# Sigmoid attention and a SiLU feed-forward: a scores-first option for visits, new orders for the opening, for FF1's products and for the places of visits

## The chip, the cores and the metric

The kernel runs on one core of a Trainium2 chip. What counts is the device time of one execution in microseconds, as the median of several runs. The core has five engines with an instruction stream each: PE (matmuls; PEld are its weight loads), DVE (vector), ACT (activations), POOL and SP (both issue DMAs here; POOL also computes). They run beside each other and wait for one another through semaphores only.

## The reference

```python
# q, k, v: (8 batches, 12 heads, 448 positions, 64)
scores = scale * np.matmul(q, k.transpose(0, 1, 3, 2)) - np.log(S)
attn = 1.0 / (1.0 + np.exp(-scores))
x = np.matmul(attn, v)            # then to (3584 tokens, 768)
h = x @ w_in                      # (768, 2048)
g = h * (1.0 / (1.0 + np.exp(-h)))
out = g @ w_out                   # (2048, 768)
```

The sigmoid takes the place of a softmax, so no row sums are needed. The kernel holds its operands in float16 and accumulates in float32.

## The kernel before

Attention is cut into 24 groups `i` of four heads, three for each batch (`i = 3*batch + n`). Each group has seven score steps `r` of 64 keys. A score step (`score_step`, L172) is four 64x64 matmuls of 448 columns that fill the four quadrants of PE, and gives one PSUM pair of banks; `sigmoid` (L178, ACT) brings it to SBUF as float16. The values of a group (`value_steps`, L188) are 7 x 4 such matmuls and read all seven sigmoids; `to_x` (L206 on DVE; L203 and L204 on DVE and ACT for the last group of batch 1) moves the result into x. In the code a unit `("s", i, r)` is a score step with its sigmoid, and `("a", i)` is a group's values with the move. The three PSUM pairs are `att0`, `att1`, `att2`; two single banks `ffp0` and `ffp1` form "pair 3".

A *visit* is a short run of such units put into the stream of feed-forward matmuls. `visit` takes the pairs that have been unused for longest, first does the "a" units, and then the "s" units; it also fires the loads and transpositions of groups to come. A score step needs its pair to have been emptied by the sigmoid, or by the move, that used it last.

The program runs in this order.

1. *Opening* (the list `INIT`). Loads, transpositions of q and k on PE (`T`, L148, copied out by DVE at L158), the scores of batch 0 and the first of batch 1, the values of batch 0 in pieces (`V`, one piece for each step), the moves to x (`X`), and the first FF1 matmuls (`F n`: n of them). `("s",)` is the next score step; these alternate between `att0` and `att1`. `("L", kind, i)` is a load by POOL's queue (kind 0 q, 1 k, 2 v; two DMAs each), `("W", s)` a quarter of w_in by the same queue. POOL has at most eight loads open at a time: each issue waits for the landing of the one eight before it. The quarters are called W0 to W3 below; FF1 needs W0 from step 0, W1 from step 24, W2 from step 48, W3 from step 72.
2. *FF1 of batch 0* (`ff1_first`, L282): 96 matmuls in eight blocks of 12, alternately in pair 3 and `att2`; after each block ACT's sigmoid (L295, L299) and a DVE multiply (L297, L300) make the gate. The list `PROGRAM` gives the steps (0 to 96) at which visits ("v") of two units stand, and where DVE forms the sums of w_in ("w", L317 to L319; "l", L323) and of x ("x" and "y", L218) that a Strassen-like scheme needs.
3. *Phases 1 to 7*. Phase `b` first does `ff1` of batch b (L350): 14 products of 12 matmuls, seven for each half `s` of the columns. `ORD[b-1]` says in which order the two halves take turns. Within a half the products alternate between two pairs X and Z; a product can start when the one before in its pair has been copied out (ACT, L381), added up (DVE, L385) or gated. Then comes the second matrix product, `ff2` (L473): 88 to 144 matmuls, through `ffp0` and `ffp1`. `PHASES[b-1]` lists the step among them at which each visit of batch b+1 stands, and how many units it has (2 or 3 near the end, 1 for the last group's values). The last visit brings the x that the next phase's FF1 begins with.

With visits of 3, 3, 3, 3, 3, 3, 3, 2, 1 units, visits 0, 1, 2, 4 and 5 hold scores only, visits 3 and 6 hold values and scores, and the last holds values only. The order is written out by hand: every engine takes its instructions in the order in which the code emits them.

```python
pairs = [p for p in used if p < n][: len(us)]
for p in pairs:
    used.remove(p)
    used.append(p)
```

Of the kernel before, what the change touches and what calls it, by code (L numbers as in the profile page):

```python
# [16 lines left out]
def kernel(  # L17
# [149 lines left out]
    def score_step(i, r, pair):  # L167
        qT, kT = qk_of(i)
        for e, j in ((0, 0), (1, 1), (0, 1), (1, 0)):
            re = slice(e * HP, (e + 1) * HP)  # L170
            cj = slice(j * HP, (j + 1) * HP)
            nc.tensor.matmul(  # L172
                att[pair][cj, e, :S], kT[re, r, cj], qT[re, :, cj], start=True, stop=True
            )
# [54 lines left out]

    used = [0, 1, 2]  # L230

    def visit(us, n=3, hold=False):

        if not hold:
            flush()
        pairs = [p for p in used if p < n][: len(us)]
        for p in pairs:
            used.remove(p)
            used.append(p)
        for u in us:  # L240
            if u[0] == "a":
                pr = pairs.pop(0)
                value_steps(u[1], pr, range(R))
                to_x(u[1], pr, hold)
                if u[1] >= 2 * NQ:
                    x_sums(slice(u[1] % NQ, u[1] % NQ + 1))
        for u in us:
            if u[0] == "s":
                pr = pairs.pop(0)
                score_step(u[1], u[2], pr)  # L250
                sigmoid(u[1], u[2], pr)
        for u in us:
            for f in events.pop(u, ()):
                f()
# [357 lines left out]
    def T(kind, i, pair):  # L612
# [3 lines left out]
            t_copy(kind, i, pair, half, dve)  # L616

    PROGRAM = (
# [6 lines left out]
    )  # L625

    INIT = (
# [13 lines left out]
    )  # L641

    us = units_of(1)
    scores = [("s", i, r) for i in range(NQ) for r in range(R)] + us
    ns = 0
    for what, *a in INIT:
        if what == "s":
            u = scores[ns]
# [17 lines left out]
    us = us[ns - NQ * R :]  # L666
# [25 lines left out]
    for n, kind, c in PROGRAM:  # L692
        ff0_steps(n - done)
        done = n
        if kind == "v":
            visit(vs[vn], 2, vn == len(vs) - 1)
            vn += 1
        else:
            acts[kind, c]()
# [1 line left out]


    PHASES = (
# [6 lines left out]
        (),  # L710
    )

# [3 lines left out]
    )  # L716

    ORD = (
# [7 lines left out]
    )  # L726

    FF2 = (
# [5 lines left out]
    for b in range(1, B):  # L734
# [15 lines left out]
        it = run()  # L750
        done = 0
        nu = 0
        for target, m in PHASES[b - 1]:
            while done < target:
                next(it)
                done += 1
            visit(us[nu : nu + m])
            nu += m
        for _ in it:
            pass  # L760
# [30 lines left out]
```

## Time and profile before

| | us |
|---|---|
| median of 4 runs | 371.49 (371.34 to 371.89) |
| the profiled execution's own time | 371.58 |
| its span from first to last instruction | 369.8 |
| opening, up to the first FF1 matmul | 0 to 30.1 |
| FF1 of batch 0 and its visits | 30.1 to 60.0 |
| phase 1 | 60.0 to 106.2 |
| phases 2, 3, 4 | 44.3 each, to 239.2 |
| phase 5 | 42.3, to 281.6 |
| phase 6 | 44.5, to 326.0 |
| phase 7 and the end | 43.8, to 369.8 |

The boundaries are the starts of each stage's first matmul in PE's timeline. Busy times come from the profiled execution, which is one run; so estimates are made against its own 371.58 us. In a timeline, the first column is the start in us, the second how long the merged run of instructions lasts, x4 how many they are, and the brackets how long the engine had been idle and what released it. The ends of matmuls are modelled and overlap the next ones, so the time that a matmul takes is read from the start of the next one.

### The profile page before, as it was taken

The page shows a single profiled execution, that of the slowest core. Times are in us where ns is not written, and L with a number is a line of the kernel's source. Part 1 is how long each engine was busy: PE and PEld are TensorE (multiplying, and loading weights), DVE is VectorE, ACT ScalarE, POOL GpSimd, SP SyncE. Part 2 cuts the span into 40 slices and gives each one's busy share as a digit, 9 for nine tenths or more (in the row PEclk, how much of TensorE's full clock was granted, in tenths as well). Part 3 has the DMA queues.
Part 4 walks back from the last instruction along what each step waited for, and adds up shares of the span by engine and source line. Part 5 has one row for each costly group of instructions (what it writes and reads, how often), then busy time and mean ns, then how long its engine had stood idle before and what let it go on. Part 6 is the DMA issues. An engine that isn't in the chain of part 4 may idle for free.

```text
span 369.8 us, 8711 instructions
## 1 busy us (share of the span) xinstructions
PE 357.2 (97%) x3594; PEld 238.9 (65%) x3594; DVE 223.1 (60%) x399; ACT 256.2 (69%) x291; POOL 159.6 (43%) x162
## 2 busy tenths in 40 slices
PE   7779999999999999999999999999999999999995
PEld 3444446965579655895549955598547965489663
DVE  2673688958765574665655755627366557436762
ACT  3989897778846797577875778467994779746100
POOL 8871430295305923169121872029631590006500
PEclk9999999999999999999999999999999999999999
DMA  8999999859897099662997449891799715130133
GB/s 145 169 178 205 228 226 188 149 124 129 143 267 158 6 171 211 162 151 38 205 183 172 101 56 203 203 209 28 102 177 225 152 17 118 29 87 2 43 87 85
DMA packets 64839, 51.13 MB, mean 138 GB/s; under 512 B 36896, under 2 KB 61728, under 8 KB 64800
## 3 DMA queue, kind: packets, MB, share of 16 engines
q1 hardware_dynamic: 48544, 35.24, 44.3%
q0 software_dynamic: 15328, 14.32, 26.6%
q10 hardware_dynamic: 928, 1.02, 0.9%
q8 instruction: 28, 0.46, 0.6%
q14 instruction: 11, 0.09, 0.1%
HBM read 45.61 MB, written 11.01 MB: 153 GB/s over the span
## 4 chain that ended last, share of the span: by engine, by line
PE 88%; ACT 5%; DVE 3%; issue 1%; DMA 1%; POOL 0%; ACTq 0%; DVEq 0%; POOLq 0%
PE ffp L473 35%; PE att L350 24%; PE att L172 9%; PE att L188 9%; PE ffp L350 6%; ACT attnT L178 5%; PE att L282 2%; PE ffp L282 2%; DMA st<-in_q_dram 1%; DVE wt L158 1%; DVE qkT L158 1%; PE att L148 0%; PE ffp L148 0%; DVE gT L300 0%; DVE gT L373 0%
## 5 line engine op out<-in xcount | busy, mean ns | idle before, releaser
L178 ACT ACTIVATE attnT<-att,bias_s 128x896 f16<-128x896 f32 x168 | 157.4, 1008 | 28.1 <-PE att L172 27.5
L371 POOL TENSOR_TENSOR gT<-attnT,gT 128x896 f16<-128x896 f32 x42 | 77.9, 1885 | 54.3 <-ACT gT L369 54.3
L126 POOL CAST st<-st 128x896 f16<-128x896 f32 x36 | 33.6, 952 | 120.2 <-DMA st<-in_k_dram 53.9
L350 PEld LDWEIGHTS <-w_in_sb 128*128 128x128 f16 x672 | 64.4, 98 | 1.6 <-issue 0.8
L350 PE MATMUL att<-xT,w_in_sb 128*128 128x224 f16 x588 | 61.2, 259 | 0.3 <-DVE gT L300 0.3
L473 PEld LDWEIGHTS <-gT 128*128 128x128 f16 x416 | 39.1, 98 | 28.7 <-issue 5.3
L381 ACT COPY attnT<-att 128x896 f32<-128x896 f32 x35 | 31.7, 906 | 37.4 <-PE att L350 37.1
L473 PEld LDWEIGHTS <-gs 128*128 128x128 f16 x384 | 34.8, 98 | 32.0 <-issue 11.5
L473 PE MATMUL ffp<-w_out_sb,gT 128*128 128x384 f16 x288 | 51.5, 326 | 0.0
L369 ACT ACTIVATE gT<-attnT 128x896 f16<-128x896 f32 x42 | 39.9, 951 | 16.2 <-DVE attnT L385 14.9
L350 PEld LDWEIGHTS <-sw 128*128 128x128 f16 x504 | 48.3, 98 | 0.1
L172 PE MATMUL att<-qkT,qkT 64*64 64x448 f16 x588 | 41.9, 358 | 4.3 <-ACT attnT L178 3.2
L385 DVE TENSOR_TENSOR attnT<-att,attnT 128x896 f32<-128x896 f32 x28 | 30.5, 1092 | 17.1 <-PE att L350 16.1
L206 DVE TENSOR_SCALAR xT<-att 128x896 f16<-128x896 f32 x21 | 22.9, 1091 | 26.5 <-PE att L188 26.5
L473 PE MATMUL ffp<-w_out_sb,gs 128*128 128x384 f16 x192 | 36.3, 327 | 0.0
L473 PE MATMUL ffp<-wt,gs 128*128 128x384 f16 x192 | 35.8, 327 | 0.0
L484 DVE TENSOR_SCALAR snap<-ffp 128x384 f32<-128x384 f32 x40 | 22.2, 555 | 21.3 <-PE ffp L473 21.3
L350 PE MATMUL att<-xT,sw 128*128 128x224 f16 x336 | 35.0, 259 | 0.0
L188 PE MATMUL att<-attnT,v 64*64 64x448 f16 x588 | 32.7, 352 | 1.3 <-DVE wt L158 0.9
L172 PEld LDWEIGHTS <-qkT 64*64 64x64 f16 x588 | 16.9, 105 | 24.4 <-issue 18.3
L487 DVE SCALAR_TENSOR_TENSOR osb<-ffp,snap 128x384 f32<-128x384 f32 x40 | 22.2, 554 | 17.2 <-PE ffp L473 17.0
L385 DVE TENSOR_TENSOR attnT<-ffp,attnT 128x448 f32<-128x448 f32 x28 | 16.1, 617 | 25.7 <-PE ffp L350 14.4
(72 smaller groups left out, 339.0 us busy)
## 6 DMA issues: line engine op xcount, KB each, us to landing
out_dram<-osb SPq DMA_DIRECT2D x48, 192.0 KB, 3.8
st<-in_k_dram SPq DMA_DIRECT2D x36, 224.0 KB, 5.0
st<-in_q_dram SPq DMA_DIRECT2D x36, 224.0 KB, 5.2
v<-in_v_dram POOLq DMA_DIRECT2D x44, 112.0 KB, 4.3
w_in_sb<-in_moe_w_in_dram POOLq DMA_DIRECT2D x4, 768.0 KB, 12.5
w_out_sb<-in_moe_w_out_dram POOLq DMA_DIRECT2D x4, 768.0 KB, 18.6
sw<-in_k_dram POOLq DMA_DIRECT2D x8, 112.0 KB, 4.3
sw<-in_q_dram POOLq DMA_DIRECT2D x8, 112.0 KB, 4.3
```

The lines of the kernel that those rows point to most:

```text
L126: nc.gpsimd.tensor_copy(st16[kind].rearrange("p r e d -> p e r d"), st32[kind].rearrange("p e (r d) -> p e r d", r=R),)
L172: nc.tensor.matmul(att[pair][cj, e, :S], kT[re, r, cj], qT[re, :, cj], start=True, stop=True)
L178: nc.scalar.activation(attnT[:, s0 : s0 + 2, :], att[pair][:, :, :S], AF.Sigmoid, bias=bias_s, scale=QKSCALE)
L188: nc.tensor.matmul(bank(pair, j)[e * HP : (e + 1) * HP, :S], vt[rj, e, r, :], attnT[rj, s0 + e, :], start=(r == 0), stop=(r == R - 1),)
L206: nc.vector.tensor_scalar_mul(x, att[pair][:, :, :S], SX)
L350: nc.tensor.matmul(o, a[:, c, (4 * s + f) * P : (4 * s + f + 1) * P], xb[:, c], start=first and c == 0 and f % 2 == 0, stop=c == KC - 1, s ...
L369: nc.scalar.activation(oo, ap, AF.Sigmoid, bias=0.0, scale=ISX)
L371: nc.gpsimd.tensor_mul(oo, ap, oo)
L381: nc.scalar.copy(as2(h[:, i, c], ap), ap)
L385: nc.vector.tensor_add(as2(h[:, i, c], ap), ap, as2(h[:, i, c], ap))
L473: nc.tensor.matmul(bank, a[:, fc], w[:, fc], start=first and fc == 0, stop=fc == KH - 1, skip_group_check=True,)
L484: nc.vector.tensor_scalar_mul(snap[i], bank, ISX)
```

## The change

`visit` gets an argument `scores_first`; with it the "s" units of a visit are emitted before its "a" units, and take the pairs in that order. A new table `SF` lists the visits that are to have it: `SF[0]` for the visits of `PROGRAM`, `SF[b]` for those of phase b. `INIT`, `PROGRAM`, `PHASES` and `ORD` get new entries; the instructions are the same in kind and number. In the opening the loads are in a different order as well (q of unit 4 ahead of its k, q of unit 5 ahead of a v load, the v load of unit 3 ahead of W1). The order of SP's queue is the same.

```diff
-    def visit(us, n=3, hold=False):
+    def visit(us, n=3, hold=False, scores_first=False):
...
-        for u in us:
-            if u[0] == "a":
+        for what in ("s", "a") if scores_first else ("a", "s"):
+            for u in us:
+                if u[0] != what:
+                    continue
                 pr = pairs.pop(0)
+                if what == "s":
+                    score_step(u[1], u[2], pr)
+                    sigmoid(u[1], u[2], pr)
+                    continue
...
     PROGRAM = (
-        (8, "v", 0), (16, "v", 0), (32, "v", 0), (38, "v", 0), (43, "w", 1),
-        (43, "v", 0), (51, "v", 0), (53, "w", 0), (58, "v", 0), (69, "v", 0),
-        (71, "w", 3), (74, "v", 0), (86, "w", 2), (89, "v", 0), (94, "v", 0),
-        (96, "l", 1), (96, "x", 0), (96, "v", 0), (96, "x", 1), (96, "x", 2),
-        (96, "f", 0), (96, "l", 0), (96, "y", 2), (96, "y", 1), (96, "y", 0),
+        (14, "v", 0), (20, "v", 0), (28, "v", 0), (36, "w", 1), (37, "v", 0),
+        (43, "v", 0), (52, "v", 0), (58, "w", 0), (59, "v", 0), (64, "v", 0),
+        (67, "w", 3), (72, "v", 0), (86, "v", 0), (93, "v", 0), (93, "w", 2),
+        (96, "x", 0), (96, "l", 1), (96, "v", 0), (96, "x", 1), (96, "x", 2),
+        (96, "y", 0), (96, "y", 2), (96, "f", 0), (96, "y", 1), (96, "l", 0),
         (96, "1", 0), (96, "2", 0),
     )
+    SF = (
+        (0, 1, 2, 3, 6, 7, 9, 10, 11), (2, 5, 7, 10), (0, 1, 2, 5), (0, 1, 2, 7, 10),
+        (1, 2, 5, 7), (4, 5, 7, 8, 9), (1, 2), (),
+    )
     INIT = (
-        ("L", 1, 3), ("s",), ("s",), ("T", 1, 1, 2), ("s",), ("s",), ("s",),
-        ("T", 0, 1, 3), ("L", 0, 3), ("L", 1, 4), ("s",), ("T", 1, 2, 2), ("s",),
-        ("L", 0, 4), ("s",), ("T", 0, 2, 3), ("s",), ("L", 2, 1), ("L", 1, 5),
-        ("T", 1, 3, 2), ("s",), ("V", 0, 2, 0), ("V", 0, 2, 1), ("s",), ("L", 2, 2),
-        ("V", 0, 2, 2), ("L", 0, 5), ("W", 0), ("W", 1), ("V", 0, 2, 3), ("V", 0, 2, 4),
-        ("T", 0, 3, 3), ("V", 0, 2, 5), ("s",), ("V", 0, 2, 6), ("X", 0, 2),
-        ("T", 1, 4, 3), ("s",), ("s",), ("W", 2), ("T", 0, 4, 2), ("s",), ("L", 2, 5),
-        ("V", 1, 3, 0), ("V", 1, 3, 1), ("L", 2, 4), ("L", 2, 3), ("s",), ("s",),
-        ("W", 3), ("T", 1, 5, 2), ("s",), ("V", 1, 3, 2), ("T", 0, 5, 2),
-        ("V", 1, 3, 3), ("s",), ("V", 1, 3, 4), ("V", 1, 3, 5), ("s",), ("s",),
-        ("V", 2, 2, 0), ("V", 2, 2, 1), ("V", 2, 2, 2), ("V", 2, 2, 3), ("V", 1, 3, 6),
-        ("s",), ("V", 2, 2, 4), ("V", 2, 2, 5), ("V", 2, 2, 6), ("s",), ("X", 1, 3),
-        ("F", 4), ("X", 2, 2, True), ("F", 4),
+        ("s",), ("s",), ("s",), ("T", 1, 1, 2), ("L", 1, 3), ("s",), ("L", 0, 3),
+        ("T", 0, 1, 3), ("s",), ("s",), ("T", 1, 2, 2), ("s",), ("s",), ("L", 0, 4),
+        ("T", 0, 2, 3), ("L", 1, 4), ("s",), ("L", 2, 1), ("T", 1, 3, 2),
+        ("T", 0, 3, 3), ("s",), ("L", 1, 5), ("V", 0, 2, 0), ("L", 0, 5), ("s",),
+        ("V", 0, 2, 1), ("L", 2, 2), ("V", 0, 2, 2), ("V", 0, 2, 3), ("W", 0),
+        ("L", 2, 3), ("V", 0, 2, 4), ("V", 0, 2, 5), ("V", 0, 2, 6), ("W", 1), ("W", 2),
+        ("s",), ("s",), ("X", 0, 2), ("s",), ("T", 1, 4, 3), ("T", 0, 4, 2), ("s",),
+        ("L", 2, 5), ("V", 1, 3, 0), ("V", 1, 3, 1), ("W", 3), ("s",), ("V", 1, 3, 2),
+        ("T", 1, 5, 2), ("s",), ("s",), ("T", 0, 5, 2), ("V", 1, 3, 3), ("s",),
+        ("V", 1, 3, 4), ("s",), ("V", 1, 3, 5), ("V", 2, 2, 0), ("V", 2, 2, 1), ("s",),
+        ("L", 2, 4), ("V", 2, 2, 2), ("V", 1, 3, 6), ("V", 2, 2, 3), ("V", 2, 2, 4),
+        ("s",), ("V", 2, 2, 5), ("s",), ("V", 2, 2, 6), ("X", 1, 3), ("F", 4), ("F", 4),
+        ("X", 2, 2, True),
     )
...
-            visit(vs[vn], 2, vn == len(vs) - 1)
+            visit(vs[vn], 2, vn == len(vs) - 1, vn in SF[0])
...
     PHASES = (
-        ((19, 3), (33, 3), (46, 3), (58, 3), (67, 3), (82, 3), (90, 3), (97, 2), (107, 1)),
-        ((19, 3), (33, 3), (47, 3), (53, 3), (62, 3), (77, 3), (89, 2), (95, 3), (107, 1)),
+        ((19, 3), (33, 3), (47, 3), (55, 3), (67, 3), (82, 3), (89, 3), (100, 2), (106, 1)),
+        ((19, 3), (33, 3), (47, 3), (53, 3), (63, 3), (78, 3), (85, 2), (93, 3), (108, 1)),
         ((19, 3), (33, 3), (48, 3), (54, 3), (63, 3), (77, 3), (85, 3), (91, 2), (98, 1)),
-        ((17, 3), (32, 3), (46, 3), (53, 3), (62, 3), (76, 3), (83, 3), (92, 2), (97, 1)),
-        ((14, 3), (23, 3), (37, 3), (40, 3), (47, 3), (58, 3), (63, 2), (67, 3), (75, 1)),
-        ((19, 3), (32, 3), (44, 3), (50, 3), (59, 3), (75, 3), (83, 3), (91, 2), (99, 1)),
+        ((18, 3), (32, 3), (47, 3), (54, 3), (63, 3), (77, 3), (84, 3), (92, 2), (99, 1)),
+        ((18, 3), (31, 3), (43, 3), (46, 3), (53, 3), (64, 3), (68, 2), (73, 3), (81, 1)),
+        ((18, 3), (32, 3), (45, 3), (51, 3), (60, 3), (74, 3), (85, 3), (92, 2), (99, 1)),
         (),
     )
     ORD = (
-        (0, 0, 1, 0, 1, 1, 0, 0, 1, 0, 1, 0, 1, 1),
-        (0, 0, 1, 1, 0, 0, 1, 0, 0, 1, 1, 0, 1, 1),
-        (0, 1, 0, 0, 1, 1, 0, 0, 1, 1, 0, 0, 1, 1),
-        (0, 0, 1, 0, 0, 1, 1, 0, 1, 1, 0, 0, 1, 1),
-        (0, 0, 1, 1, 0, 1, 0, 0, 1, 0, 1, 0, 1, 1),
-        (0, 0, 1, 1, 0, 1, 0, 1, 0, 0, 1, 0, 1, 1),
-        (0, 0, 1, 1, 0, 0, 1, 0, 1, 0, 1, 0, 1, 1),
+        (0, 0, 0, 1, 1, 1, 0, 0, 1, 1, 0, 0, 1, 1),
+        (0, 0, 1, 1, 0, 1, 0, 0, 0, 1, 1, 0, 1, 1),
+        (0, 1, 0, 0, 1, 0, 1, 1, 0, 1, 0, 0, 1, 1),
+        (0, 0, 1, 0, 0, 1, 1, 0, 1, 0, 1, 0, 1, 1),
+        (0, 0, 1, 1, 0, 1, 0, 1, 0, 1, 0, 0, 1, 1),
+        (0, 1, 0, 0, 1, 0, 1, 1, 0, 1, 0, 0, 1, 1),
+        (0, 0, 1, 0, 1, 0, 0, 1, 0, 1, 1, 0, 1, 1),
     )
...
-            visit(us[nu : nu + m])
+            visit(us[nu : nu + m], scores_first=nv in SF[b])
```

The step at which a visit stands counts FF1 matmuls in `PROGRAM` and FF2 matmuls in `PHASES`.

More of the change, by code (lines that the diff above doesn't have):

```diff
@@ L246, in visit @@
                     x_sums(slice(u[1] % NQ, u[1] % NQ + 1))
[L247 to L251, printed above, removed]
         for u in us:
@@ L752 @@
         nu = 0
-        for target, m in PHASES[b - 1]:
+        for nv, (target, m) in enumerate(PHASES[b - 1]):
             while done < target:
```

## The prediction

> **What bounds the kernel now.** I read the page's busy row first, then the windows of the stretches between the stages, then PE's and ACT's timelines in the stretches where PE is not full.
>
> ```profile
> PE 357.2 (97%) x3594; PEld 238.9 (65%) x3594; DVE 223.1 (60%) x399; ACT 256.2 (69%) x291; POOL 159.6 (43%) x162
> ```
>
> PE is busy nearly throughout, but a busy PE is not PE at its peak, so stages are compared:
>
> ```profile
> 7.90:30.10 22.20, 17.36 (x317) 10.18 (x317) 13.40 (x24) 19.98 (x22) 16.36 (x28) 1.00 1.18 176
> 30.10:60.00 29.90, 29.14 (x260) 12.87 (x256) 19.56 (x32) 26.27 (x34) 8.83 (x12) 1.00 1.19 218
> 194.90:239.20 44.30, 44.30 (x450) 30.66 (x448) 27.01 (x50) 32.25 (x36) 20.11 (x18) 1.00 0.74 148
> 239.20:281.60 42.40, 41.70 (x427) 28.95 (x425) 21.91 (x41) 32.23 (x36) 20.13 (x18) 1.00 0.72 138
> ```
>
> Columns after the length: busy PE, PEld, DVE, ACT, POOL. Phase 4 (third line) is pure PE. Phases 2, 3 and 4 last 44.3 us each and hold the same matmuls: nothing is to be gained there, only lost. The opening (first line) is ACT's: 20.0 of 22.2 us. Phase 5 has the same 21 sigmoids on ACT but 24 FF2 matmuls fewer (88 for 112), so its PE waits. Where:
>
> ```profile
> 257.69 0.57 PE L172 MATMUL att<-qkT,qkT 64*64 64x448 f16 x8
> 258.43 0.38 PE L172 MATMUL att<-qkT,qkT 64*64 64x448 f16 x4 [0.17 <-DVE gT L373]
> ...
> 260.32 0.57 PE L172 MATMUL att<-qkT,qkT 64*64 64x448 f16 x8
> 261.05 0.38 PE L172 MATMUL att<-qkT,qkT 64*64 64x448 f16 x4 [0.16 <-ACT attnT L178]
> ```
>
> A score step of four quadrant matmuls takes 0.19-0.21 us start to start (258.43 would have been 258.10). The gaps in brackets look small because matmul ends are modelled; by starts the two stalls cost 0.34 and 0.33 us.
>
> ACT in the opening, and POOL's loads behind it:
>
> ```profile
> 17.69 1.01 ACT L178 ACTIVATE attnT<-att,bias_s 128x896 f16<-128x896 f32 x1 [0.31 <-PE att L172]
> 19.28 1.01 ACT L178 ACTIVATE attnT<-att,bias_s 128x896 f16<-128x896 f32 x1 [0.58 <-PE att L172]
> 20.53 5.50 ACT L178 ACTIVATE attnT<-att,bias_s 128x896 f16<-128x896 f32 x6 [0.25 <-PE att L172]
> 26.73 4.60 ACT L178 ACTIVATE attnT<-att,bias_s 128x896 f16<-128x896 f32 x5 [0.70 <-PE att L172]
> ```
> ```profile
> 19.72 2.52 POOL L554 DMA_DIRECT2D w_in_sb<-in_moe_w_in_dram  x3
> ...
> 29.91 0.60 POOL L119 DMA_DIRECT2D v<-in_v_dram  x1 [4.69 <-DMA w_in_sb<-in_moe_w_in_dram]
> 33.70 0.84 POOL L554 DMA_DIRECT2D w_in_sb<-in_moe_w_in_dram  x1 [3.20 <-DMA w_in_sb<-in_moe_w_in_dram]
> ```
>
> Back to back, sigmoids start 0.89 us apart (5.50 for six, each 1.0 long). ACT idles four times waiting for a score that PE issued late. The POOL waits date the landings of w_in's pieces: W0 29.6, W1 33.4, so 3.8 us apiece. PE's first FF1 matmul stands at 30.09, only 0.5 us after W0.
>
> **What the skill says.** "TensorE: Matmul & The Clock Gate", section "Architectural detail: the array is 16× 32×32, not 1× 128×128": PE pulls only weight loads ahead, ACT and DVE are strict FIFO; so an instruction that waits holds all behind it. The trace agrees: the waits of L172 stop the FF2 stream. "DMA: Bandwidth & Descriptors", section "Anatomy of one DMA — SWDGE (gpsimd) path", prices a transfer at 2.0 us plus bytes/436 GB/s. A w_in piece is 128x6x512 floats, 1.57 MB: 3.6 us of movement; the trace shows 3.8 between landings.
>
> **The change, part by part.**
>
> *Scores ahead of values: nothing.* The option re-orders only a visit that holds both kinds. In the batch-0 program those are visits 4 and 8; the list has 0-3, 6, 7, 9-11. In phases 1 to 6 they are visits 3 and 6; the lists (2,5,7,10), (0,1,2,5), (0,1,2,7,10), (1,2,5,7), (4,5,7,8,9), (1,2) never name them. Not one instruction moves by it.
>
> *Opening (the list INIT).* I place each score by the rules above: its bank is free 0.05 us after the sigmoid before last; its own sigmoid starts 0.43 us after it (17.26 to 17.69) or when ACT is free; a transposition pair takes 0.58 us on PE, its two copies 1.16 us on DVE. Up to s1.1 ACT runs full in both. Now both transpositions of unit 3 stand ahead of s1.2, and q's half landed only at 16.06, so s1.2 goes from 15.63 to 16.65 and its sigmoid from 16.31 to 17.07 (a new gap of 0.76). But the value steps and transpositions that delayed s1.4 by 0.58 and s2.4 by 0.70 no longer do: s1.3 17.96, s1.4 18.88, s1.5 19.77, s1.6 20.66, s2.0 21.80, s2.1 22.83, s2.2 24.06, s2.4 25.87, s3.1 29.43 instead of 30.32. ACT gains 0.9 us; PE reaches FF1 at 29.2. W0 has the same eight loads ahead of it, so it lands at about 29.6: FF1 starts at 29.65 instead of 30.09. Gain 0.44, the rest hidden by W0.
>
> *FF1 of batch 0 (the list PROGRAM).* 96 matmuls at 0.187 us; a visit of two scores costs 0.50, with values 1.9, plus 0.1 on re-entry. The first visit is now at step 14, past the first gate, so ACT does the gate first and is no further ahead at the next scores (s3.4 34.6 for 34.9). Stalls for a bank: before 0.52 (39.35 to 40.06), 0.5 (41.83), 0.27 (47.02), 0.2 (57.98); now by the same rules 0.43 (s3.5), 0.2 (a3), 0.29 (s5.0), 0.32 (s5.2). Summing from 29.65 I get steps 24, 43, 72, 96 at 35.9, 40.7, 50.5, 57.7 and the last value's end at 59.2 instead of 60.0: gain 0.85 in all with the 0.44. One more v load (0.57 us each half) goes ahead of W1, so it lands at 34.6-35.0, needed at 35.9. The DVE sums at step 36 need W2 (W1 and 3.8 us more, 38.5-38.9) and are reached at 40.7. Step 93's sums end near 58.0, before the last value.
>
> *FF1 of phase 1 (ORD).* Before:
>
> ```profile
> 61.25 1.41 PE L350 MATMUL ffp<-xT,sw 128*128 128x224 f16 x12
> 62.93 1.31 PE L350 MATMUL att<-xT,w_in_sb 128*128 128x224 f16 x12 [0.26 <-DVE gT L300]
> ```
>
> A product takes 1.15 us, here 1.68: the third one waited for batch 0's last gate multiply on DVE. Now the third product reuses its own bank after the copy (0.26 latency + 0.91 + 0.05 against 1.15: stall 0.07) and the gate's bank comes fourth. The multiply itself is moved behind four x sums (4 x 0.19), so it ends just then (0.05); "1,1,1" costs 0.07. Gain 0.25.
>
> *ORD elsewhere.* "0,0,0" in phase 2 falls on products whose bank a DVE pair of 2 x 0.62 frees, half by half: ready at 0.86 and 1.40, needed at 1.15 and 1.73. In the other orders at least two products lie between a bank's uses, or one where the evacuation is that pair. Zero; range 0 to 0.3 lost over six phases.
>
> *PHASES.* Moves of one to three steps change nothing in phases that had no stall. In phase 5 visits go 14, 23, 37, 40 ... 75 to 18, 31, 43, 46 ... 81. The first visit comes at 255.33+18x0.163+0.09 = 258.35, so DVE's multiply (end 258.38) is done when its third score comes. 13 and 12 steps (2.1, 2.0 us) plus the visit's 0.69 then cover three sigmoids (2.68 to 2.8). By the opening's rules what is left is 0.05, 0.1, 0.15+0.28 (visit 3), 0.3 (visit 5), 0.06: 0.9 us. Before, phase 5 stood 1.9 us over the loss of phases 2 to 4 (start-to-start sum less the undisturbed spacing). Gain 1.0; range 0.5 to 1.2. What is late next is the last value: 7 FF2 matmuls (1.14 us) and two thirds of the first product (0.77) cover x's move (0.2 + 1.09 + 0.05): enough by 0.6. In phase 2 the last visit at 108 leaves 0.65+0.77 = 1.42 against 1.34: enough by 0.1. Phase 6: visit 45 for 44 saves 0.1.
>
> *Sum.* 0.85+0.25+1.0 = 2.1. The profiled execution took 371.58 us (span 369.8), the median 371.49; 2.1 off either gives 369.5 and 369.4. Less than 0.2% (0.74 us) could not be told from no change.
>
> **Rivals.** (A) The opening is held by w_in. If a w_in piece behind small loads takes what W0 took (6.4 us after the load ahead of it, not 3.8), W1 lands at 30.8+6.4 = 37.2: 1.3 late at step 24, of which later stalls give back some 0.4. For it: W0's 6.4; against it: W0 had an empty transfer ahead. Gain 1.2: 370.3. (B) Phase 5 only trades stalls: ACT has 21 x 0.89 = 18.8 us of sigmoids between 258.85 and the last value at 279, 20.1 us, so 1.3 us of slack; small gaps on ACT eat it and the last value waits for its seventh sigmoid. With 0.5 gained there, 0.3 lost in ORD, 0.4 of the opening's 0.85 and nothing in phase 1: gain 0.6, 370.9. (C) Slower: W1's issue is held by the limit of eight open loads until W0 lands (as the v load at 29.91 was), and takes W0's 9.9 us from issue: 39.8, 3.9 after step 24. It decides from a landing past 38.7 (35.9+2.1+0.74) and gives 373.3. Against it: W1 is only the third after W0, its slot's former load landed at 20.9. (D) W0 itself comes earlier, since one PE wait fewer stands ahead of it: up to 0.4 more, and fewer stalls: 368.6.
>
> **How the numbers follow.** Forecast 0.58, A 0.17, B 0.13 (0.04 of it still faster by 0.2%), C 0.06, D 0.06. Faster 0.58+0.17+0.04+0.06 = 0.85, same 0.09, slower 0.06. The range goes from D's side, 368.2, to B's, 371.1.
>
> **What would show it.** FF1's first matmul at 29.6; ACT's gaps in the opening 0.76 at 16.3 and then under 0.4; the last value of batch 0 ending near 59.2; phase 1's FF1 16.4 long instead of 16.7; phases 2 to 4 still 44.3; phase 5 41.3 for 42.3. Wrong if a stall stands at step 24, if phases 2 to 4 lengthen, or if the first two stalls of phase 5 remain.

## The result and the profile after

| | median, us | runs, lowest to highest | ratio to before (95% interval) |
|---|---|---|---|
| before | 371.75 | 59, 371.17 to 374.66 | |
| changed | 370.55 | 38, 369.36 to 372.09 | 0.9964 (0.9956 to 0.9973) |

The change takes 0.36% off by the ratio, 1.3 us (the two medians lie 1.2 apart), where 2.1 was forecast. Single executions of the changed kernel spread over 2.7 us, and its profiled one, with 371.70 us (span 369.8), is among the slowest: as a whole it is no faster than the profiled one of before (371.58). So it is read stage by stage. Windows of the changed kernel, cut at its own first matmuls of each stage; after the length come the busy times of PE, PEld, DVE, ACT and POOL, then TensorE's granted clock, the DMA share and GB/s:

```profile
7.90:30.60 22.70, 18.18 (x317) 10.88 (x318) 14.08 (x25) 20.57 (x23) 16.42 (x26) 0.92 1.11 163
30.60:60.50 29.90, 29.14 (x261) 12.73 (x257) 18.33 (x31) 26.62 (x34) 8.66 (x12) 1.00 1.19 218
60.50:107.35 46.85, 46.10 (x460) 31.35 (x457) 37.46 (x66) 32.99 (x37) 20.79 (x18) 1.00 0.86 149
195.90:240.30 44.40, 44.40 (x450) 30.74 (x449) 26.80 (x50) 32.19 (x36) 20.11 (x18) 1.00 0.75 151
240.30:281.70 41.40, 41.09 (x426) 28.96 (x424) 22.10 (x40) 32.35 (x36) 20.07 (x18) 1.00 0.69 127
```

The reader is to see four things. The opening is longer than before (22.7 for 22.2), at a clock of 0.92. FF1 of batch 0 lasts 29.9 as before. Phase 1 has grown from 46.2 to 46.85. Phase 5 is down from 42.4 to 41.4. PE's timeline of phase 5 shows that its first two stalls are gone; the lines at 259.46 and 262.37 are the first two visits, their twelve matmuls in one piece each, where both were cut by a stall in the kernel before (at 258.43 and 261.05):

```profile
257.74 1.46 PE L474 MATMUL ffp<-w_out_sb,gT 128*128 128x384 f16 x8
259.04 0.49 PE L474 MATMUL ffp<-wt,gT 128*128 128x384 f16 x2
259.46 0.76 PE L172 MATMUL att<-qkT,qkT 64*64 64x448 f16 x12
260.15 1.15 PE L474 MATMUL ffp<-wt,gT 128*128 128x384 f16 x6
...
262.37 0.82 PE L172 MATMUL att<-qkT,qkT 64*64 64x448 f16 x12
```

ACT's timeline of the opening, whose gaps before were 0.31, 0.58, 0.25 and 0.70:

```profile
8.65 2.81 ACT L178 ACTIVATE attnT<-att,bias_s 128x896 f16<-128x896 f32 x3 [0.62 <-PE att L172]
11.76 1.01 ACT L178 ACTIVATE attnT<-att,bias_s 128x896 f16<-128x896 f32 x1 [0.30 <-PE att L172]
13.16 6.63 ACT L178 ACTIVATE attnT<-att,bias_s 128x896 f16<-128x896 f32 x7 [0.39 <-PE att L172]
20.10 4.91 ACT L178 ACTIVATE attnT<-att,bias_s 128x896 f16<-128x896 f32 x5 [0.32 <-PE att L172]
25.21 6.62 ACT L178 ACTIVATE attnT<-att,bias_s 128x896 f16<-128x896 f32 x7 [0.20 <-PE att L172]
```

The late gaps have shrunk as forecast (0.32 and 0.20 are left). But there are new ones at 11.76 and 13.16, where no order was meant to cost anything, and the first sigmoid is at 8.65 (before: 8.29). In the window from 9.5 to 13.0 the granted clock was 0.51 in this execution and 1.00 in that of before. The two new gaps fall under this clock: there the fourteen matmuls of a transposition took 0.96 us (the first line, of the changed kernel), where they take 0.58 in an execution at full clock (the second line, of the run `after_t_early` below), so the scores came late.

```profile
10.23 0.96 PE L148 MATMUL att<-ident,sw 128*64 128x128 f16 x14
8.60 0.58 PE L148 MATMUL att<-ident,sw 128*64 128x128 f16 x14
```

Most of the new loss in phase 1 is one stall. PE waits at step 48 of FF2 (one matmul after the visit at 47) for DVE's copy of the product that ended at step 40. The expectations below call this place step 41.

```profile
86.19 0.76 PE L172 MATMUL att<-qkT,qkT 64*64 64x448 f16 x12
86.88 0.34 PE L474 MATMUL ffp<-w_out_sb,gT 128*128 128x384 f16 x1
87.89 1.30 PE L474 MATMUL ffp<-wt,gT 128*128 128x384 f16 x7 [0.67 <-DVE snap L485]
```

DVE's timeline at that place, where the copy (L485) stands behind the two sums of w_out (T3, L433):

```profile
83.53 3.82 DVE L433 TENSOR_TENSOR w_out_sb<-w_out_sb 128x1536 f16<-128x1536 f16 x2
87.29 0.55 DVE L485 TENSOR_SCALAR snap<-ffp 128x384 f32<-128x384 f32 x1
```

and POOL's at the same time, its sixth gate multiply:

```profile
83.93 2.60 POOL L372 TENSOR_TENSOR gT<-attnT,gT 128x896 f16<-128x896 f32 x1
```

The same pair of sums in the kernel before, with POOL's sixth multiply, which began ahead of them:

```profile
82.29 1.88 POOL L371 TENSOR_TENSOR gT<-attnT,gT 128x896 f16<-128x896 f32 x1
83.40 2.46 DVE L432 TENSOR_TENSOR w_out_sb<-w_out_sb 128x1536 f16<-128x1536 f16 x2
85.80 0.55 DVE L484 TENSOR_SCALAR snap<-ffp 128x384 f32<-128x384 f32 x1
```

### The profile page after: what moved, and what is told of

Read it like the earlier page. It is cut to its first block, busy times and chain, and to the rows that moved or that the text cites. A ratio compares the mean times of both kernels' runs of the same rounds, so it can differ in the third digit from the quotient of the medians.

```text
span 369.8 us, 8710 instructions
## 1 busy us (share of the span) xinstructions
PE 357.3 (97%) x3594; PEld 239.2 (65%) x3594; DVE 225.1 (61%) x399; ACT 256.8 (69%) x291; POOL 160.2 (43%) x162
## 3 DMA queue, kind: packets, MB, share of 16 engines
q10 hardware_dynamic: 928, 1.02, 0.8%
## 4 chain that ended last, share of the span: by engine, by line
PE 88%; ACT 5%; DVE 3%; issue 2%; DMA 1%; POOL 0%; ACTq 0%; DVEq 0%; POOLq 0%
PE ffp L474 35%; PE att L351 24%; PE att L172 9%; PE att L188 8%; PE ffp L351 7%; ACT attnT L178 5%; PE ffp L283 3%; PE att L283 2%; DMA st<-in_q_dram 1%; DVE wt L158 1%; DVE w_out_sb L433 1%; PE att L148 1%; PE ffp L148 1%; DVE qkT L158 1%; DVE osb L546 0%
## 5 line engine op out<-in xcount | busy, mean ns | idle before, releaser
L372 POOL TENSOR_TENSOR gT<-attnT,gT 128x896 f16<-128x896 f32 x42 | 78.7, 1904 | 52.3 <-ACT gT L370 52.3
L485 DVE TENSOR_SCALAR snap<-ffp 128x384 f32<-128x384 f32 x40 | 22.2, 556 | 21.4 <-PE ffp L474 21.4
L488 DVE SCALAR_TENSOR_TENSOR osb<-ffp,snap 128x384 f32<-128x384 f32 x40 | 22.2, 555 | 15.0 <-PE ffp L474 14.9
```

The costliest lines, as they stand in the source:

```text
L372: nc.gpsimd.tensor_mul(oo, ap, oo)
L485: nc.vector.tensor_scalar_mul(snap[i], bank, ISX)
```

## The experiments

In the tables below, a phase's length is from its first matmul to that of the next; a loss is the sum of start-to-start times of a kind of matmul less their undisturbed spacing. Times of one batch of runs are compared with runs of the kernel before on the same chip. The lists of `SF` name no visit that holds both scores and values, so the option `scores_first` moves no instruction and has no part in what follows.

**One: the parts alone.** `phase5_only` is the kernel before with the new row of `PHASES` for phase 5; `opening_only` has the new `INIT` and `PROGRAM`.

```diff
-        ((14, 3), (23, 3), (37, 3), (40, 3), (47, 3), (58, 3), (63, 2), (67, 3), (75, 1)),
+        ((18, 3), (31, 3), (43, 3), (46, 3), (53, 3), (64, 3), (68, 2), (73, 3), (81, 1)),
```

> The kernel before, with the new places of phase 5's visits alone. The prediction priced this at 1.0 us of gain (0.5 to 1.2); the trace of the changed kernel shows phase 5 at 41.47 us for 42.33, so 0.86. Theory 1 (the gain in phase 5 is kept to the end): phase 5 lasts 41.3 to 41.5 us, every other phase as before, and the time is 0.8 to 1.0 us below the kernel before (ratio 0.9973 to 0.9979). Theory 2 (it is given back in phase 6, whose FF1 waits for the last value, now seven matmuls ahead of it): phase 6 grows by as much and the ratio is 1.000.

> The kernel before, with the new opening and the new order inside FF1 of batch 0, and the old ORD and PHASES. Predicted gain of this part 0.85 us. Theory 1 (half clock): PE stands idle for 1.1 us ahead of the third score; in some executions its clock is then granted at one half for 3.4 us of the opening (as in the changed kernel's profile, 9.5 to 13.0 us), which costs 0.5 to 1.2 us. Then the executions fall in two groups, those with a mean clock of 0.997 or more about 0.5 us below the kernel before, those with 0.995 or less about 0.4 us above it. Theory 2 (the loads): the last value of batch 0 ends later than in the kernel before whatever the clock is, since the loads of w_in and q land later; then the time is 0 to 0.6 us above the kernel before and does not go with the clock. Ratio: theory 1 0.998 to 1.000, theory 2 1.000 to 1.002.

| kernel | median us (runs) | ratio (95%) | phase 1 starts | phase 1 | FF1 loss in it | phase 5 | phase 6 |
|---|---|---|---|---|---|---|---|
| before (profile) | 371.59 (45) | | 60.01 | 46.24 | 0.62 | 42.33 | 44.49 |
| phase5_only | 371.44 (13) | 0.9998 (0.9989 to 1.0007) | 60.08 | 46.25 | 0.62 | 41.47 | 44.98 |
| opening_only | 372.29 (22) | 1.0015 (1.0005 to 1.0025) | 59.32 | 46.99 | 1.37 | 42.33 | 44.49 |

By the medians `phase5_only` can't be told from the kernel before, and `opening_only` is 0.15% slower; neither brings what was priced. The traces name a reason for each. In `phase5_only` phase 5 gains 0.86, but phase 6 gives 0.49 back, so 0.37 is left (experiment two comes back to why the median doesn't show it). Phase 6's second product uses the pair `ffp`, and waits for DVE's copy of FF2's last product out of it (L545). In DVE's queue this copy stands behind the move of the last value's x and its sums. PE's timeline, then DVE's:

```profile
280.76 1.31 PE L350 MATMUL att<-xT,w_in_sb 128*128 128x224 f16 x12
282.41 1.31 PE L350 MATMUL ffp<-xT,sw 128*128 128x224 f16 x12 [0.33 <-DVE osb L545]
```
```profile
281.62 0.27 DVE L218 TENSOR_TENSOR xT<-xT,xT 128x224 f16<-128x224 f16 x1
281.80 0.55 DVE L545 TENSOR_SCALAR osb<-ffp 128x384 f32<-128x384 f32 x1
```

In `opening_only` phase 1 starts 0.7 earlier and loses 0.75 more in FF1, because the third product of the old order uses the bank of batch 0's last gate, whose multiply now stands behind four more x sums. Phase 4 is 0.17 longer as well in this profile, for no reason that was looked into; the profiled execution (371.80) is one of the fastest of its 22, so most of the median's 0.7 is not explained by it. PE's timeline:

```profile
60.57 1.42 PE L350 MATMUL ffp<-xT,sw 128*128 128x224 f16 x12
62.99 1.21 PE L350 MATMUL att<-xT,w_in_sb 128*128 128x224 f16 x11 [1.00 <-DVE gT L300]
```

So the rows of `ORD` for phases 1 and 6 seem not to be a separate edit: they pay for the two others. Two kernels test this, with the new row of `ORD` for phase 6 and for phase 1 added.

```diff
 # phase56: phase5_only and
-        (0, 0, 1, 1, 0, 1, 0, 1, 0, 0, 1, 0, 1, 1),
+        (0, 1, 0, 0, 1, 0, 1, 1, 0, 1, 0, 0, 1, 1),
 # opening_ord1: opening_only and
-        (0, 0, 1, 0, 1, 1, 0, 0, 1, 0, 1, 0, 1, 1),
+        (0, 0, 0, 1, 1, 1, 0, 0, 1, 1, 0, 0, 1, 1),
```

> The kernel before with the new visits of phase 5 and the new order of phase 6's products, nothing else. Theory 1 (with the old order phase 6's second product waits for the x sums of the last value, as in phase5_only, 0.49 us; with the new one another product stands between): phase 5 41.47 us, phase 6 44.49 us or less, time 0.8 to 1.0 us below the kernel before, ratio 0.9973 to 0.9980. Theory 2 (the wait only moves to the third product): phase 6 44.9, ratio 0.9985 to 0.9990 as in phase5_only.

> The kernel before with the new opening, the new order inside FF1 of batch 0 and the new order of phase 1's products. opening_only lost 1.37 us in phase 1's FF1 with the old order of products. Theory 1: this FF1 loses 0.3 us now, and FF2 stalls 0.6 to 1.0 at step 41; phases 0 and 1 together end 0.4 to 0.5 us earlier than in the kernel before (106.25), ratio 0.9985 to 0.9993. Theory 2 (ORD has no part in it): FF1 still loses over 1 us, ratio 1.000 to 1.002.

`phase56`: 371.10 (10 runs; before 371.61), ratio 0.9984 (0.9971 to 0.9997); phase 6 lasts 44.48, so by the profile phase 5's 0.86 stays, as the first expectation had it. (The expectation names the x sums; by the trace above it is the copy behind them.) The median gains 0.5, between the two ranges. `opening_ord1`: 371.38 (14 runs), 0.9991 (0.9977 to 1.0005): FF1 of phase 1 now loses 0.26, as expected, and yet phase 1 ends at 106.23 (before: 106.25) and the kernel can't be told from that before. Its FF2 in phase 1 loses 1.45 (before: 0.91), and in its profile the opening itself was held by a late load, that of q of unit 3, which the new order puts ahead of score s1.2:

```profile
14.91 0.58 PE L148 MATMUL att<-ident,st 128*64 128x128 f16 x14
16.67 0.58 PE L148 MATMUL ffp<-ident,st 128*64 128x128 f16 x14 [1.18 <-DMA st<-in_q_dram]
```

**Two: why the opening is late in some executions.** The new order has the transposition of k of unit 1 behind the third score, not ahead of it. `after_t_early` puts it ahead again in the changed kernel, `before_t_late` puts it behind in the kernel before; `after_again` is the changed kernel once more.

```diff
 # after_t_early
-        ("s",), ("s",), ("s",), ("T", 1, 1, 2), ("L", 1, 3), ("s",), ("L", 0, 3),
+        ("s",), ("s",), ("T", 1, 1, 2), ("s",), ("L", 1, 3), ("s",), ("L", 0, 3),
 # before_t_late
-        ("L", 1, 3), ("s",), ("s",), ("T", 1, 1, 2), ("s",), ("s",), ("s",),
+        ("L", 1, 3), ("s",), ("s",), ("s",), ("T", 1, 1, 2), ("s",), ("s",),
```

> The changed kernel with one step moved back: the first transposition of unit 1's k stands ahead of the third score again, so that PE has work while it waits for the first sigmoid. Theory 1 (half clock): no execution, or fewer than one in ten, has a mean clock of 0.995 or less (a third of the changed kernel's runs have), and the median is 370.0 to 370.3 us, 0.3 to 0.5 below the changed kernel's. Theory 2 (the loads): clock or not, the median stays at 370.4 to 370.7.

> The kernel before with this one step alone: the first transposition of unit 1's k behind the third score, so that PE is idle for about 0.7 us more. Theory 1 (half clock): a quarter or more of its executions show a mean clock of 0.995 or less and are 0.5 to 1.2 us longer than the others; ratio over all 1.000 to 1.002. Theory 2 (the order alone costs nothing and the clock does not follow it): no more executions with a low clock than in the kernel before, ratio 0.9995 to 1.0005.

> The changed kernel once more, on the same chip as the other three. Theory 1: executions with a mean clock over 0.996 lie at 370.1 to 370.3 us, and a profile of such an execution shows the start of phase 1 at 59.3, phase 1 46.5 to 46.9 long, phase 5 41.47 and phase 6 44.33; executions with half clock in the opening lie 0.6 to 1.0 us higher. Theory 2 (the opening of the changed kernel is slow for other reasons than the clock): the start of phase 1 is at 60 us or later although no half clock shows before it.

`after_t_early` 370.23 (7 runs), 0.9963 (0.9950 to 0.9976); `before_t_late` 371.78 (14), 1.0002 (0.9994 to 1.0010); `after_again` 370.80 (22), 0.9975 (0.9964 to 0.9987). The place of this transposition is not shown to be a cause: the time of the kernel before stays the same with it, and the intervals of the changed kernel with and without it overlap. The low clocks that the first expectations looked for do not sort by it either (2 of 7 executions of `after_t_early`, where fewer than one in ten was expected; 5 of 14 of `before_t_late` against 9 of 45 of before, too few to tell). The profile of `after_t_early`, however, shows the opening as forecast (FF1's first matmul at 29.45, straight after W0's landing at 29.41; phase 1 from 59.35). That of `after_again` shows the changed kernel's order 1 us later at full clock, as its second expectation had it; here W0 is late, and its phase 1, with 47.57, is the longest of all:

```profile
29.19 0.38 PE L188 MATMUL att<-attnT,v 64*64 64x448 f16 x4
30.49 0.74 PE L283 MATMUL ffp<-xT,w_in_sb 128*128 128x448 f16 x3 [0.92 <-DMA w_in_sb<-in_moe_w_in_dram]
```

A last kernel of this kind, `t_early_q3`, is `after_t_early` with score s1.2 ahead of the transposition of q of unit 3.

```diff
-        ("T", 0, 3, 3), ("s",), ("L", 1, 5), ("V", 0, 2, 0), ("L", 0, 5), ("s",),
+        ("s",), ("T", 0, 3, 3), ("L", 1, 5), ("V", 0, 2, 0), ("L", 0, 5), ("s",),
```

> The changed kernel with T1,1 ahead of the third score and with s1.2 ahead of q's transposition of unit 3, so that no score stands behind the load of q of unit 3. Theory 1 (W0's landing bounds the start of FF1 in any case): ACT's gap of 0.76 at 16.3 is gone, FF1 still starts at 29.4 to 29.6, phase 1 at 59.3, time 370.2 as after_t_early within 0.2. Theory 2 (late loads of q are what makes the opening slow in many executions): the median falls to 369.8 and the spread narrows.

It took 370.86 (7 runs, 370.25 to 371.43; before 371.70), 0.9973 (0.9962 to 0.9984): neither expectation of the time is met. Its ACT has no gap at s1.2, but the first sigmoid started at 8.96 instead of 8.35, and all that follows is 0.5 to 0.6 later (FF1 29.98, phase 1 59.89). Over the fourteen profiles the first sigmoid starts between 8.02 and 8.96; with the old opening FF1's first matmul then stands at 29.90 to 31.00, with the new one at 29.42 to 30.67.

No run sets out to take the causes apart, but the profiles can be sorted. The half clock stands in the opening of four: from 9.55 for 3.41 us in the changed kernel, from 10.96 for 3.41 in `old_opening`, from 8.06 and 8.93 for 6.83 in `gate_dve` and `after_t3_late`. These are the four latest starts of FF1, 30.59 to 31.00. In `t_early_q3` a transposition at 9.25 takes 0.96, the length at half clock; its first matmuls are slow, and its first sigmoid is the latest. Of the other nine, `after_again` (30.49, W0) and `opening_ord1` (29.90, q) were held by loads. The rest have 29.90 to 30.16 with the old opening, and 29.42 and 29.45 with the new one. In the changed kernel's profile the two gaps of ACT under the half clock account for 0.9 of the 1.14 by which its FF1 starts later than that of `after_t_early`.

The same shows in whole executions, sorted afterwards by their mean granted clock (over the whole span, so it does not tell where the clock was low):

| kernel | 0.995 or less: runs, median us | more: runs, median us |
|---|---|---|
| before (batch of `phase5_only`; its other batches 372.4 to 372.5, and 371.6) | 9, 372.59 | 36, 371.56 |
| phase5_only | 5, 372.04 | 8, 371.09 |
| opening_only | 8, 372.77 | 14, 371.96 |
| before_t_late | 5, 372.10 | 9, 371.61 |
| phase56 | 5, 371.55 | 5, 370.67 |
| changed | 14, 371.12 | 24, 370.25 |
| after_again | 6, 370.89 | 16, 370.80 |
| after_t_early | 2, 370.67 | 5, 370.11 |
| old_opening | 2, 370.96 | 3, 370.23 |

A low clock goes with 0.5 to 1.0 us more in all rows but that of `after_again`, in the kernel before as in the changed one. So it accounts for a part of the spread, but not for the gain that is missing from the forecast: in either column `changed` lies 1.3 to 1.5 below before, no more. (`after_again` lies only 0.8 below at the higher clock, so other causes, such as its late loads, count as well.) The clock also blurs the parts: `phase5_only` and `phase56` have a larger share of such executions than the kernel before, and at the higher clock they gain 0.5 and 0.9, near the 0.37 and 0.86 of their traces. `opening_only` splits by the clock, as its first expectation had it, but both of its groups are longer than those of before, so its loss is not the clock's alone. The groups are small, and which executions get the low clock was not controlled.

**Three: what phase 1 gives back.** In every profile the stretch from FF1's first matmul to phase 1 is 29.90 to 29.92 long, so `PROGRAM` neither gains nor loses. But with the new opening and the new order of phase 1's FF1, FF2 of phase 1 loses 0.5 to 1.4 more than before (with the old order, `opening_only`, FF1 itself has lost that time by then), mostly in the stall at step 48 shown above. `after_t3_late` moves the two T3 sums behind the copy that waits for them.

```diff
-            if n == 0:
-                w_sum(T3, B22, B12)
             ahead(2)
             return
...
         copy(0, X)
         flush()
+        if n == 1:
+            w_sum(T3, B22, B12)
```

> The changed kernel, with DVE's two sums for T3 moved from behind the first row block of phase 1's FF2 to behind the copy that opens the second one. In the profiles of the changed kernel and of after_t_early that copy stood behind these sums, which took 3.9 and 3.7 us for 2.5 before, and PE waited 0.8 to 1.0 us at FF2 step 41 of phase 1. Theory 1 (the opening's gain is taken back there, by the sums ahead of the copy): the stall is gone, phase 1 lasts 45.8 to 45.9 us, and the time is 0.6 to 0.9 us below the changed kernel on the same chip, 369.3 to 369.7. Theory 2 (any late instruction of DVE's queue stalls phase 1, since its additions and POOL's multiplies started late): the stall moves a few steps on and the time is within 0.2 us of the changed kernel.

370.56 (7 runs), 0.9971 (0.9958 to 0.9984), no better than the changed kernel. The stall at step 48 is gone, but steps of 0.47 (at 92.47) and 0.59 (at 95.71) from one matmul to the next take its place, and FF2's loss is 1.55, as the second expectation had it. The sums stay long (1.63 and 1.68); they now stand beside POOL's two casts, which took 3.06 together where two take 1.82 elsewhere.

Why are they long? The times of POOL's sixth multiply and of DVE's first sum are counted here from the start of phase 1; the profiles stand in the order of the former:

| profile | phase 1 starts | POOL's sixth multiply | DVE's first sum | the two T3 sums | FF2 loss |
|---|---|---|---|---|---|
| old_opening (below) | 60.92 | 21.70 | 23.02 | 1.39 + 0.95 | 0.91 |
| before | 60.01 | 22.28 | 23.39 | 1.60 + 0.95 | 0.91 |
| phase56 | 59.89 | 22.57 | 23.39 | 1.88 + 0.95 | 0.91 |
| after_t_early | 59.35 | 23.21 | 23.04 | 1.02 + 2.64 | 1.50 |
| opening_only | 59.32 | 23.27 | 24.14 | 1.83 + 0.95 | 0.91 |
| changed | 60.49 | 23.44 | 23.04 | 1.25 + 2.64 | 1.89 |
| after_again | 60.39 | 24.30 | 23.04 | 2.12 + 2.63 | 2.34 |

Where the multiply has begun ahead of the first sum, only that sum is longer than 0.95, and FF2 loses 0.91. Where it begins after it, the second sum takes 2.64 and FF2 loses more. In `opening_only` the multiply is as late, but so are the sums, since FF1 has lost 0.75.

POOL's multiplies stand behind its casts of unit 7's k and q, and these wait for landings (POOL's timeline of `after_t_early`):

```profile
70.40 0.93 POOL L126 CAST st<-st 128x896 f16<-128x896 f32 x1 [17.19 <-DMA st<-in_k_dram]
72.42 0.93 POOL L126 CAST st<-st 128x896 f16<-128x896 f32 x1 [1.09 <-DMA st<-in_q_dram]
73.32 11.83 POOL L372 TENSOR_TENSOR gT<-attnT,gT 128x896 f16<-128x896 f32 x6
```

PE came to phase 1 0.66 earlier than in the kernel before, and its FF1 there lost 0.36 less, so DVE's sums begin 1.01 earlier (82.39 for 83.40). But k and q of unit 7 landed 0.3 later. These loads did not move up with PE; why they landed when they did was not tested. So POOL's sixth multiply is still to come when DVE starts its sums. The Trainium skill, "SBUF — State Buffer", section "SBUF: two separate sides", says that an operation of POOL that reads SBUF and one of DVE with two SBUF inputs take a shared port pair by an exclusive lock: the one that starts first keeps it for its whole instruction, and the other blocks. The trace agrees: the first sum (82.39 to 83.4) holds back POOL's sixth multiply (from 82.56, 2.60 long instead of 1.88), which holds back the second sum (from 83.33, 2.64 instead of 0.95).

```profile
82.39 3.58 DVE L433 TENSOR_TENSOR w_out_sb<-w_out_sb 128x1536 f16<-128x1536 f16 x2
83.33 2.64 DVE L433 TENSOR_TENSOR w_out_sb<-w_out_sb 128x1536 f16<-128x1536 f16 x1
```

The sum of the time alone and of what is left of the other engine's operation gives the length that the trace shows, in this profile and in every other where these sums meet multiplies alone: thirteen of the fourteen, each sum and each multiply within 0.15 us. DVE's gate multiply from PSUM has one SBUF input, and took its normal 1.08 beside a POOL multiply. So the engines here wait for one another through more than semaphores, which the start of this document leaves out, and the blocked operation is shown as long and busy, not as waiting.

`gate_dve` tests that: it is `after_t_early` with the fourth gate of phase 1 multiplied on DVE, so that POOL is done earlier.

```diff
     GP = (
-        (1, 1, 1, 1, 1, 1), (1, 1, 1, 1, 1, 1), (1, 1, 1, 1, 1, 1), (1, 1, 1, 1, 1, 1),
+        (1, 1, 1, 0, 1, 1), (1, 1, 1, 1, 1, 1), (1, 1, 1, 1, 1, 1), (1, 1, 1, 1, 1, 1),
```

> The changed kernel with T1,1 ahead of the third score (as in after_t_early) and with one of the six gate multiplies of phase 1 given from POOL to DVE, where DVE idles for about 1.07 us; POOL's chain of multiplies then ends near 83.2 instead of 85.15, before most of DVE's two T3 sums. Theory 1 (DVE's sum and POOL's multiply slow each other, and that makes the copy at FF2 step 41 late): the two sums take 0.95 to 1.25 each instead of 1.0 and 2.6, the stall of 0.77 at 86.5 is gone, phase 1 lasts 45.7 to 46.0 instead of 46.48, time 369.6 to 369.8. Theory 2 (the sum is long for another reason, such as its operands' place): it still takes 2.6 and phase 1 stays at 46.4 to 46.5. Theory 3 (DVE has no room for the multiply): FF1 of phase 1 loses 0.3 to 0.8 more, and the time is no better than 370.2.

The two sums now take 1.02 and 0.95, and the stall at step 48 is gone (DVE's timeline):

```profile
74.99 2.64 DVE L374 TENSOR_TENSOR gT<-attnT,gT 128x896 f16<-128x896 f32 x1
77.55 1.08 DVE L386 TENSOR_TENSOR attnT<-att,attnT 128x896 f32<-128x896 f32 x1
...
84.71 1.89 DVE L433 TENSOR_TENSOR w_out_sb<-w_out_sb 128x1536 f16<-128x1536 f16 x2
86.54 0.55 DVE L485 TENSOR_SCALAR snap<-ffp 128x384 f32<-128x384 f32 x1
```

But the multiply itself has two SBUF inputs and meets the same lock: 2.64 long in the first line, where an idle stretch of about 1.07 had been reckoned to hold it. DVE is late for the copy of the first FF2 product, and PE's next matmul starts only at 80.15, 0.84 after the one before it:

```profile
80.15 0.65 PE L474 MATMUL ffp<-wt,gT 128*128 128x384 f16 x3 [0.51 <-DVE snap L485]
```

Phase 1 lasts 47.05, the time is 370.99 (22 runs), 0.9974 (0.9964 to 0.9984). So it is shown that the long sums come from POOL's multiply beside them, and the lengths are those of the lock that the page describes. The cure only moved it, as the third of the expectations had it, in FF2 rather than in FF1.

**Four: is the new opening worth anything?** `old_opening` is the changed kernel with `INIT` and `PROGRAM` of before; `old_opening_gate` has the edit of `gate_dve` as well.

> The changed kernel with INIT and PROGRAM of the kernel before; the new ORD, PHASES and the option stay. Theory 1 (the new opening's gain is given back in phase 1, and in many executions it does not come at all; what counts is phases 5 and 6): phase 1 starts at 59.9 to 60.1 as before, lasts 46.0 to 46.3, phase 5 41.47, phase 6 44.33; the time is 370.6, as that of the changed kernel within 0.2, with a narrower spread. Theory 2 (the opening carries part of the median's gain): 371.0 to 371.1, 0.3 to 0.5 above the changed kernel.

> old_opening with the same gate multiply given to DVE. Theory 1: the sums that took 1.6 and 0.95 take 0.95 each, but in this order no product waited for them, so phase 1 gains 0 to 0.2 and the time is that of old_opening within 0.2. Theory 3 (DVE has no room): 0.3 to 0.8 slower than old_opening.

`old_opening` took 370.72 (5 runs, 370.14 to 371.07), 0.9967 (0.9955 to 0.9979); `old_opening_gate` 370.23 (6 runs, 370.00 to 371.14), 0.9960 (0.9947 to 0.9973). The changed kernel had 0.9964 and 0.9975 in its two groups of runs: without the new opening it is as fast within the intervals. An estimate from the first group: the new opening brings 0.1 us, give or take 0.55. The 0.85 that was forecast for `INIT` and `PROGRAM` lies outside, a few tenths do not. In the profile of `old_opening` phase 1 lasts 45.86, the shortest of all: FF1 loses 0.24 instead of 0.62 by its new order, and FF2 loses 0.91 as before. Its start is late in that execution (60.92, outside what was expected, with the half clock from 10.96), so the length and not the start carries the reading. In `old_opening_gate` phase 1 is longer (46.74), with steps of 0.55 and 0.65 from one matmul to the next at the copy and the score behind DVE's multiply, so the gate's move is a loss there by the trace; that its median is nevertheless the lower one is within the spread of five and six runs. No kernel that ran is shown to be faster than the changed one.

## Why the prediction was partly right

The direction, the range and the largest term held; the sum was 2.1 and the median gained 1.3. The account is from the profile of `after_t_early` (the changed kernel but for one transposition, 370.11 us in an execution with an undisturbed opening, so a good one) against that of before (371.58):

| term of the prediction | forecast gain | measured |
|---|---|---|
| opening, to FF1's first matmul | 0.44 | 0.64 |
| FF1 of batch 0 (`PROGRAM`) | 0.41 | 0.02 |
| FF1 of phase 1 | 0.25 | 0.36 |
| FF2 of phase 1 | not priced | -0.59 |
| phases 2 to 4 (`ORD` elsewhere) | 0 | 0.00 |
| phase 5 | 1.0 | 0.86 |
| phase 6 | 0.1 | 0.16 |
| phase 7 and the end | not priced | 0.13 |
| sum | 2.2, given as 2.1 | 1.58 (spans: 1.57; execution times: 1.47) |

- *Scores ahead of values: nothing.* Right.
- *Opening.* Right where the loads come in time: FF1 at 29.45 for the 29.65 forecast, bounded by W0 as said. But the forecast took the landings of one execution as fixed. The gap of 0.76 at 16.3 that it placed by the landing of q came about so in `after_again` alone (0.75); where q landed sooner it is 0.2 to 0.4 at full clock, and in `opening_ord1`, where q landed at 16.54, it is 1.44. And it took the clock as full: in the changed kernel's own profile, under the half clock, FF1 stood at 30.59.
- *PROGRAM, 0.41 of the 0.85.* Wrong by 0.39. The stalls of the new order, 0.49, 0.27, 0.25 and 0.41 in `after_t_early`, add up to 1.42 where 1.24 was reckoned, and those of the old one to 1.41 where 1.49 was. The visits trade stalls one for one. That is 0.26 of the 0.39; the rest stands in no stall, and was not found. ACT is busy for 26 to 27 of the 29.9 us in either order, which fits a stretch that ACT sets, but no run tested that.
- *FF1 of phase 1.* The mechanism was right. What the prediction didn't say is that the same row is a must: with the old row, the new `PROGRAM` loses 0.75 more there.
- *The step that failed by omission* is phase 1's FF2. The prediction priced phase 1's FF1 and left FF2 at its old length; it asked what is late next for phase 5 alone. PE gained on a stream of loads that did not gain with it, POOL's multiplies fell later against PE, and DVE and POOL then locked each other out. This returned 0.59, of the 0.66 that the opening and FF1 of batch 0 bring and the 0.36 of phase 1's FF1; 0.98 in the changed kernel's own profile, and 1.43 in that of `after_again`.
- *Phases 5 and 6.* Right: 1.02 of the 1.1. The trace of `phase5_only` adds that 0.49 of it hangs on phase 6's new row of `ORD`.
- *Rivals.* A and C did not happen: W1 landed at 34.4. D's earlier W0 showed in the good openings by 0.2. B's 0.4 for the opening and phase 1 together is what this profile shows (0.66 less the 0.23 that phase 1 loses), but by luck: B gave no cause for it, and its own cause, that phase 5 trades stalls, did not happen.

So what the median gains is close to phases 5 and 6 (1.02) and FF1 of phase 1 (0.36). That the opening adds less than forecast on the median is what `old_opening` shows; whether it adds a few tenths or nothing stays open, and so does what makes the loads late and the clock fall in some executions.

## What to carry to other kernels

When a stage is made to end earlier, ask of the next one which of its inputs come by transfers that will not move up, and which engine waits for these; a gain ahead of a fixed stream is given back at the first such wait. Look for DVE operations with two SBUF operands that can meet an operation of POOL on SBUF (here multiplies, and casts too): a shift of less than a microsecond decides whether they meet, and then each waits for what is left of the other. An order that gains in one phase may hang on the order in the next, so parts of such a change should be tried in the pairs that belong together. And where executions of one kernel differ by as much as the change under study, sort them by the granted clock before medians are compared.

## What the runs showed of the hardware that was not expected

- DVE's sum of 128x1536 float16 values took 0.95 us alone and up to 2.64 beside POOL's multiply, which itself went from 1.88 to 2.60 (2.75 in `gate_dve`).
- TensorE's granted clock was 0.51 from 9.5 to 13.0 us in the changed kernel's profile. The Trainium skill, "TensorE: Matmul & The Clock Gate", section "What's actually happening", has the clock halved after an idle window of about 3.4 us. The length agrees (3.41 us, or twice that). But in the 3.4 us ahead of it PE was not idle throughout: 1.58 of 3.42 us were busy, at full clock, and 1.7 to 2.1 in the three other profiles. The window in this execution, and the one ahead of it:

```profile
9.50:13.00 3.50, 3.29 (x44) 2.01 (x43) 1.71 (x4) 2.97 (x4) 2.06 (x5) 0.51 1.23 188
6.13:9.55 3.42, 1.58 (x30) 0.87 (x29) 1.42 (x3) 1.96 (x3) 3.42 (x6) 1.00 1.24 189
```

- The same loads land at different times from one execution to the next: in the two profiles of the changed kernel, W1 at 35.3 and 36.5 us, the first quarter of w_out at 52.1 and 53.5, k of unit 7 at 71.6 and 72.8. Over all fourteen profiles the last two range from 50.1 to 53.5 and from 69.5 to 72.8, a spread that a single profile does not show.
